# Order and place of VectorE work in the first two tiles of a retention block with a maxout feed-forward: scores behind conversion, weight sums sooner, w_out's sums off GpSimd

## The chip, the cores and the metric

The kernel runs on one core of one Trainium2 chip. A core has TensorE (matrix products, into the banks of PSUM), VectorE (in the profile DVE), ScalarE (ACT), GpSimd (POOL) and SyncE (SP), which here only issues DMAs. Each engine works through its own queue in order; they wait for each other by semaphores. The metric is device microseconds of one execution, as the median of several.

## The reference

Retention over (8, 8, 576, 64) inputs, whose output, seen as 4608 tokens of 512 features, goes into a maxout feed-forward of width 768:

```python
gamma = 1.0 - 2.0 ** (-5.0 - np.arange(H, dtype=np.float32))
Dmat = np.where(rel >= 0, gamma[:, None, None] ** rel[None, :, :], 0.0)
ret = scores * Dmat[None, :, :, :]          # scores = q k^T / sqrt(D)
attn = np.matmul(ret, v)                    # -> x: (B*S, H*D)
h = np.maximum(np.maximum(x @ w1, x @ w2), x @ w3)
out = h @ w_out
```

The weights arrive in float64. The kernel computes in float32, and converts them on the chip, from the bits.

## The kernel before

**Tiles.** The 4608 tokens are nine tiles of 512 tokens, each of four blocks of 128. `ffn(t)` (L818) is the feed-forward of tile t as a generator. The loop at the end (L979) runs it in twelve portions and, ahead of each, the steps that `steps(t + 1)` names for it: loads, transposes, `scores`, `state`, `values` of the blocks of the next tile. So TensorE's queue has the retention of tile t+1 between the products of tile t. All orders are written out by this program; nothing reorders them later.

**Tile 0** uses plain products, since the weights come in meanwhile. `units` (L482) are pairs (fp, i): fp is one of three pairs of 128-wide blocks of the hidden features, i one of the three weights. `up_plain` (L781) multiplies, and its `maximum` takes the result into h, on VectorE for i > 0. `convert(n)` runs n steps of `convert_all` (L616). A step issues one or a few of: the exponent's bits on VectorE (L632) and the mantissa's low half on ScalarE (L634); two ScalarE steps on the exponent (L640, L643) with the fraction's bits on VectorE (L641); the whole mantissa (L646); the sign (L650); and the product (L658), which is the float32 weight and which issues the loads of later pieces (`load_weights`). Pieces are worked in an overlapped order: the exponent step of a piece stands ahead of the sign and product of the piece before it. In the second unit, just behind the first block's products, `scores`, `state` and `keep` of block 4 are called (L829 to L832). `scores` (L277) issues the products of q and k to TensorE and the multiplication by a causal mask (L291, shown as L203) to VectorE; `keep` (L358) issues the new state there.

**From tile 1 on** both products use sums. The up products use a scheme with twenty products for each fp (`PRODUCTS`, L67), made of sums of x (`X_SUMS`) and of the weights (`W_SUMS`). The weight sums are made once: 19 VectorE subtractions or additions for each fp (L470), those of fp 0 at the end of tile 0, those of fp 2 and 1 during tile 1. They stand in the list `chores`. Work of the retention and sums of x stand in `urgent`. In `up` (L735) the chains A to E accumulate in PSUM banks; ScalarE copies the value of a chain after certain products (`part<-a` and so on, L747), and VectorE joins them (`JOINS`, L750). Chains C, D and E use two banks in turn, so D takes the bank of E, and the next E that of C; the joins that read e and c straight from PSUM free them.

For each TensorE step of `up` (40 for each fp: two for each product), `ffn` decides at L866 to L869 what VectorE gets next: an urgent step at step % 4 == 1, and at step % 4 == 3 if many wait; else, on even steps, one chore. The order of fp is 0, 2, 1.

**The down products** (`downs`, L531) use seven products in the banks x, y and z, called dx, dy and dz in the profile. They need sums of h (H, L527 to L529, part of them on GpSimd) and of w_out (To): T1 = b12 - b11 (L512), T2 = b22 - T1 (L513), b12 = b22 - b12 in place (L516), T4 = b21 - T2 (L517), each for three fp. T1 is used in product 5, T2 in product 6, b12 in product 7 and T4 in product 4. The order of the products is 1, 2, 6, 7, 5, 4, 3. The sums of w_out are made once, in tile 1, behind product 1 (L879). There is a step of the loop in `ffn` for each product; behind product 2 stands the sum that gives osb (L576).

Of the kernel before, what the change touches and what calls it, by code (L numbers as in the profile page):

```python
# [45 lines left out]
ALU = mybir.AluOpType  # L46
# [17 lines left out]
            b21 = b21 - b41, b42 = b42 - n5, b22 = b22 - b21, n6 = b31 + n2, b32 = b22 - b32, n8 = b12 - n4,  # L64
# [17 lines left out]
def kernel(  # L82
# [14 lines left out]
    nc = tc.nc  # L97
# [8 lines left out]
    CPT = NT // C  # L106
# [21 lines left out]
    def half(j):  # L128
        return slice(D * j, D * (j + 1))
# [31 lines left out]
    def start_of(g):  # L161
        r = -g * C % S
        return r if r < C else None
# [23 lines left out]
    late, chores, urgent, scaling, spread = {}, deque(), deque(), deque(), []  # L187

    def scale(n=1):
        for _ in range(min(n, len(scaling))):  # L190
            scaling.popleft()()  # L191

    def chore(n=1):
        for _ in range(n):
            if urgent or chores:
                (urgent or chores).popleft()()

    def soon(step):

        if spread:  # L200
            urgent.append(step)
        else:
            step()  # L203
# [73 lines left out]
    def scores(g):  # L277
        chore(len(urgent))
        scale(len(scaling))
        if g >= BY_CHUNKS:  # L280
            chunk_scores(g)
            return
        qT, kT = qks[g]["q"], qks[g]["k"]
        s = [ps_r.tile([C, NP, C], FP32, tag="r", name=f"s{j}") for j in range(2)]
        for p in range(NP):
            for j in range(2):
                r = slice(D * j, D * (j + 1))
                nc.tensor.matmul(s[j][:, p, :], lhsT=kT[r, p, :], rhs=qT[r, p, :], start=True, stop=True)
        for j in range(2):
            st = sts[g, j] = att.tile([C, NP, C], FP32, tag=f"m{j}", name="st", bufs=2 + j)  # L290
            soon(partial(nc.vector.tensor_tensor, st[:], s[j][:],  # L291
                         masks[start_of(g)][:].unsqueeze(1).to_broadcast([C, NP, C]), op=ALU.mult))

    def begins(g):
        return g + 1 < NG and start_of(g + 1) != 0
# [51 lines left out]
    def state(g):  # L347

        kr = raws["k", g]
        kvs[g] = None  # L350
        if begins(g):
            r = start_of(g) or 0
            kvs[g] = ps_r.tile([P, NP, D], FP32, tag="r", name="kv")
            for h in range(H):
                nc.tensor.matmul(kvs[g][half(h % 2), h // 2, :], lhsT=kr[r:, h, :], rhs=vds[g][r:, h, :],
                                 start=True, stop=True)

    def keep(g):  # L358
        factor = gs[:].unsqueeze(2).to_broadcast([P, NP, D])

        def step(t, kv):
            if start_of(g) is not None:
                nc.vector.tensor_tensor(t[:], kv[:], factor, op=ALU.mult)
            else:
                nc.vector.tensor_tensor(t[:], kv[:], states[g][:], op=ALU.add)
                (nc.gpsimd if g < CPT - 2 else nc.vector).tensor_tensor(t[:], t[:], factor, op=ALU.mult)

        if begins(g):
            t = states[g + 1] = ppool.tile([P, NP, D], FP32, tag="part", name="state")
            soon(partial(step, t, kvs[g]))  # L370
# [111 lines left out]
    units = [(fp, i) for fp in range(NF // 2) for i in range(3)]  # L482
# [21 lines left out]
    def sums_of_outs():  # L504

        pool = late["pool"]
        lo, hi = slice(0, DM // 2), slice(DM // 2, DM)
        b11, b12, b21, b22 = (w_out[:, :, e, r] for e in range(2) for r in (lo, hi))
        t1, t2, t4 = (pool.tile([P, NF // 2, DM // 2], FP32, name=f"To{n}")[:] for n in (1, 2, 4))

        def on_vector(fp):
            nc.vector.tensor_tensor(t1[:, fp], b12[:, fp], b11[:, fp], op=ALU.subtract)  # L512
            nc.vector.tensor_tensor(t2[:, fp], b22[:, fp], t1[:, fp], op=ALU.subtract)  # L513

        def on_gpsimd(fp):
            nc.gpsimd.tensor_tensor(b12[:, fp], b22[:, fp], b12[:, fp], op=ALU.subtract)  # L516
            nc.gpsimd.tensor_tensor(t4[:, fp], b21[:, fp], t2[:, fp], op=ALU.subtract)  # L517

        late["sums of T"] = [partial(on, fp) for on in (on_vector, on_gpsimd) for fp in (0, 2, 1)]
        late["T"] = {1: b11, 2: b21, 3: b22, 4: t4, 5: t1, 6: t2, 7: b12}  # L520
        late["S"] = {n: pool.tile([P, NF // 2, NH], FP32, name=f"H{n}") for n in (1, 2, 3, 4)}

# [201 lines left out]
    def late_room():  # L724
        pool = late["pool"]
        late["W"] = [pool.tile([P, NF, P], FP32, name=f"n{n}") for n in range(1, 9)]
        late["X"] = {n: pool.tile([P, NH], FP32, name=n)[:] for n in sorted({x[0] for x in X_SUMS})}
# [3 lines left out]
    def convert(n):  # L731
        for _ in range(n):
            next(converting, None)
# [66 lines left out]
    def first_ups(h):  # L800

        g = CPT - 1
        rest0, copy0 = up_plain(0, h, 0, 0, g * C)
        convert(2)
        state(g)
        convert(2)
        values([g])
        keep(g)
        convert(2)
        rest1, copy1 = up_plain(0, h, 1, 0, g * C)  # L810
        convert(2)
        for step in (rest0, copy0, rest1, copy1):
            step()
        decay(CPT)
        transposes(CPT)
        convert(4)

    def ffn(t):  # L818

        h = hpool.tile([P, NF, NT], FP32, tag="h", name="h")  # L820
        if t == 0:
            for fp, i in units:
                if (fp, i) == units[0]:
                    first_ups(h)
                    yield
                    continue
                for fb in (2 * fp, 2 * fp + 1):
                    maximum, = up_plain(t, h, fb, i)
                    if (fp, i, fb) == (*units[1], 0):  # L829
                        scores(CPT)  # L830
                        state(CPT)
                        keep(CPT)  # L832
                    if (fp, i) == units[-1] and fb % 2:
                        maximum()
                        convert(2)
                    else:
                        convert(4 if (fp, i) == units[1] else 2)
                        maximum()
                yield
            convert(3)  # L840
            for fb, _ in enumerate(downs_plain(t, h)):
                convert(2 if fb < 2 else 4 * len(pieces))
                if fb == 2:
                    while_converting.close()
                    late["pool"] = ctx.enter_context(tc.tile_pool(name="late", bufs=1))
                    late_room()
                    sums_of_outs()
                    weight_sums(0)
                elif fb == 3:
                    chore(len(chores))  # L850
                if fb in (1, 3):
                    yield
            yield
            return
        order = (0, 2, 1)
        if t == 1:
            spread.append(True)
            weight_sums(2)
            weight_sums(1)
        total = len(order) * 2 * len(PRODUCTS)  # L860
        count = parts = 0
        for fp in order:
            while fp not in summed_fp:
                chore()
            for step, _ in enumerate(up(t, h, fp)):
                if step % 4 == 1 or step % 4 == 3 and len(urgent) > (2 if t == 1 else 6):  # L866
                    chore(len(urgent) > 0)
                elif step % 2 == 0 and chores:
                    chores.popleft()()  # L869
                if step % 3 == 2:  # L870
                    scale()
                count += 1
                if count * (NF // 2 * 3) >= (parts + 1) * total:
                    parts += 1
                    yield
            sums_of_hidden(h, fp)
        chore(len(urgent))
        for n, _ in enumerate(downs(t, h, order)):
            if t == 1 and n == 0:  # L879
                for step in late["sums of T"]:  # L880
                    step()
            chore(4)
            scale(2)
            if n in (1, 3):
                yield
        yield
# [92 lines left out]
    for t in range(N // NT):  # L979
        work = ffn(t)  # L980
        for todo in steps(t + 1):
            for step in todo:
                step()
            next(work, None)
# [51 lines left out]
```

## Time and profile before

| what | us |
|---|---|
| median of three runs | 753.45 (753.13 to 753.48) |
| the profiled execution | 753.01 |
| its span, first to last instruction | 751.3 |
| TensorE busy | 743.1 |
| VectorE busy | 518.7 |
| ScalarE busy | 327.3 |
| GpSimd busy | 71.4 |
| tile 1, start of its up products to that of the next tile's | 123.97 to 205.5 |
| tile 2 | 205.5 to 284.4 |

Times in the trace are microseconds from the first instruction. PE is TensorE's products and PEld its weight loads, which run ahead of the products. The clock granted to TensorE is at full speed throughout. Busy shares are means over stages; the waits have to be read where they occur. The ends of TensorE's instructions in a trace are modelled, so a wait shows in full between the starts of weight loads rather than as idle time of PE. A row's line is that of the call which records the instruction; work that goes through `soon` or a list may carry the line where the list is worked off.

### The profile page before, as it was taken

The page shows a single profiled execution, that of the slowest core. Times are in us where ns is not written, and L with a number is a line of the kernel's source. Part 1 is how long each engine was busy: PE and PEld are TensorE (multiplying, and loading weights), DVE is VectorE, ACT ScalarE, POOL GpSimd, SP SyncE. Part 2 cuts the span into 40 slices and gives each one's busy share as a digit, 9 for nine tenths or more (in the row PEclk, how much of TensorE's full clock was granted, in tenths as well). Part 3 has the DMA queues.
Part 4 walks back from the last instruction along what each step waited for, and adds up shares of the span by engine and source line. Part 5 has one row for each costly group of instructions (what it writes and reads, how often), then busy time and mean ns, then how long its engine had stood idle before and what let it go on. Part 6 is the DMA issues. An engine that isn't in the chain of part 4 may idle for free.

```text
span 751.3 us, 16659 instructions
## 1 busy us (share of the span) xinstructions
PE 743.1 (99%) x6768; PEld 615.1 (82%) x6768; DVE 518.7 (69%) x878; ACT 327.3 (44%) x657; POOL 71.4 (10%) x91
## 2 busy tenths in 40 slices
PE   9999999999999999999999999999999999999998
PEld 7645546888788888888888888888888888888887
DVE  3898899898846765686667746775667656763662
ACT  3764533554145433644254335542554255414441
POOL 3000000002300100011010101010101010100000
PEclk9999999999999999999999999999999999999999
DMA  9996842504252514241333224242514151000001
GB/s 229 239 226 140 225 92 72 99 12 85 62 94 41 100 37 96 48 81 48 80 77 68 61 66 90 35 81 67 102 24 91 44 94 35 2 29 29 1 0 57
DMA packets 230206, 59.31 MB, mean 79 GB/s; under 512 B 210801, under 2 KB 228849, under 8 KB 230129
## 3 DMA queue, kind: packets, MB, share of 16 engines
q1 hardware_dynamic: 228720, 57.91, 35.6%
q8 instruction: 53, 0.87, 0.5%
q10 hardware_dynamic: 1408, 0.33, 0.2%
q14 instruction: 25, 0.20, 0.1%
HBM read 48.76 MB, written 9.44 MB: 77 GB/s over the span
## 4 chain that ended last, share of the span: by engine, by line
PE 90%; DVE 6%; SPq 2%; DMA 1%; issue 1%; ACT 0%; POOL 0%; DVEq 0%; POOLq 0%
PE a L762 18%; PE b L762 15%; PE dx L559 11%; PE c L762 8%; PE up L786 6%; PE dz L559 6%; PE d L762 5%; PE e L762 5%; PE sk L310 3%; PE down L773 3%; PE dy L559 2%; PE o L427 2%; PE o L434 1%; DVE part L750 1%; SPq L241 1%; DVE h L750 1%
## 5 line engine op out<-in xcount | busy, mean ns | idle before, releaser
L750 DVE TENSOR_TENSOR part<-part 128x512 f32<-128x512 f32 x168 | 116.0, 690 | 104.5 <-ACT part L747 102.0
L747 ACT COPY part<-b 128x512 f32<-128x512 f32 x120 | 70.3, 586 | 151.8 <-PE b L762 151.4
L750 DVE TENSOR_TENSOR h<-h,part 128x512 f32<-128x512 f32 x120 | 83.7, 698 | 29.5 <-ACT h L747 25.1
L747 ACT COPY part<-a 128x512 f32<-128x512 f32 x96 | 56.3, 586 | 51.2 <-PE a L762 50.8
L762 PE MATMUL a<-s,w 128*128 128x256 f32 x288 | 73.9, 379 | 0.0
L762 PE MATMUL b<-s,n 128*128 128x256 f32 x288 | 73.9, 379 | 0.0
L191 ACT ACTIVATE vraw<-vraw,gk 128x64 f32<-128x64 f32 x208 | 65.4, 346 | 0.5 <-DMA vraw<-in_v_dram 0.4
L786 PE MATMUL up<-xT,w 128*128 128x512 f32 (+2 forms) x160 | 64.2, 554 | 1.0 <-DVE w L658 1.0
L762 PEld LDWEIGHTS a<-s,w 128*128 128x128 f32 x288 | 54.7, 190 | 7.4
L762 PEld LDWEIGHTS b<-s,n 128*128 128x128 f32 x288 | 54.7, 190 | 7.4
L786 PEld LDWEIGHTS up<-xT,w 128*128 128x128 f32 x160 | 28.5, 190 | 31.3 <-issue 26.7
L327 POOL TENSOR_TENSOR s<-s,gs_of 64x512 f32<-64x512 f32 x21 | 22.3, 1062 | 318.1 <-DVE s L325 161.8
L762 PE MATMUL c<-xT,w 128*128 128x256 f32 x192 | 51.3, 389 | 0.0
L762 PE MATMUL d<-s,w 128*128 128x256 f32 x192 | 49.8, 380 | 0.0
L529 POOL TENSOR_TENSOR H<-h 128x256 f32<-128x256 f32 x24 | 20.2, 844 | 309.7 <-DVE h L750 305.3
L762 PE MATMUL b<-xT,n 128*128 128x256 f32 x192 | 49.3, 379 | 0.0
L559 PE MATMUL dx<-To,H 128*128 128x256 f32 (+1 forms) x204 | 45.4, 371 | 1.0 <-DVE To L513 1.0
L762 PE MATMUL e<-xT,w 128*128 128x256 f32 x192 | 45.4, 379 | 0.0
L762 PE MATMUL a<-xT,n 128*128 128x256 f32 x192 | 45.4, 379 | 0.0
L559 PEld LDWEIGHTS dx<-To,H 128*128 128x128 f32 x204 | 36.5, 190 | 6.6 <-DVE To L513 1.8
L762 PEld LDWEIGHTS e<-xT,w 128*128 128x128 f32 x192 | 36.5, 190 | 5.4 <-issue 0.5
L762 PEld LDWEIGHTS a<-xT,n 128*128 128x128 f32 x192 | 36.5, 190 | 5.0
(124 smaller groups left out, 1291.8 us busy)
## 6 DMA issues: line engine op xcount, KB each, us to landing
bits<-in_moe_w_dram SPq DMA_DIRECT2D x36, 256.0 KB, 6.0
out_dram<-osb SPq DMA_DIRECT2D x35, 256.0 KB, 2.1
kraw<-in_k_dram SPq DMA_DIRECT2D x32, 256.0 KB, 3.3
vraw<-in_v_dram SPq DMA_DIRECT2D x32, 256.0 KB, 3.9
qraw<-in_q_dram SPq DMA_DIRECT2D x224, 32.0 KB, 2.3
kxraw<-in_k_dram SPq DMA_DIRECT2D x224, 32.0 KB, 2.2
bits<-in_moe_w_out_dram SPq DMA_DIRECT2D x6, 512.0 KB, 5.5
qraw<-in_q_dram SPq DMA_DIRECT2D x6, 256.0 KB, 5.2
```

What stands on the lines that cost most here:

```text
L191: scaling.popleft()()
L241: nc.sync.dma_start(t[row:row + m], src[b, :, pos:pos + m, :].rearrange("h p d -> p h d"))
L310: nc.tensor.matmul(s[half(c), h, :], lhsT=kT[half(c), h, :], rhs=qT[half(c), h, :], start=True, stop=True)
L327: nc.gpsimd.tensor_tensor(new, new, factor, op=ALU.mult)
L427: nc.tensor.matmul(o[m][half(c), n, u, :], lhsT=vds[g][half(m), h, :], rhs=sts[g][half(m), h, :], start=n == 0 and u == 0, stop=place(g, m ...
L529: urgent.append(lambda: (pool(s3, a11, a21, op=ALU.subtract), pool(s4, a12, s2, op=ALU.subtract)))
L559: nc.tensor.matmul(o, lhsT=hS[n](fp)[:, m * P:(m + 1) * P], rhs=late["T"][n][:, fp, cols], start=first and fp == order[0] and (m == 0 or l ...
L747: nc.scalar.copy(of[step], ps[step[0]][:])
L750: nc.vector.tensor_tensor(of[dst], a, b, op=op)
L762: nc.tensor.matmul(ps[chain][:, e, :], lhsT=factor(w, 2 * fp + e), rhs=xS[t][x], start=n == 1 and e == 0, stop=ends, skip_group_check=True)
L773: nc.tensor.matmul(b[:], lhsT=h[:, fb, m * P:(m + 1) * P], rhs=w_sb["out", fb], start=(fb == 0), stop=(fb == NF - 1))
L786: nc.tensor.matmul(ps[:, a:b], lhsT=w_sb[i, fb][:, dc * P:(dc + 1) * P], rhs=xT[t][:, dc, a:b], start=dc == 0 and a == 0, stop=dc == NDC - ...
```

## The change

Three edits, all to the order or the engine of work that is there already.

1. In the second unit of tile 0, block 4's `scores`, `state` and `keep` are called behind the conversion steps and the maximum instead of ahead of them. TensorE's, ScalarE's and SP's queues keep their order; on VectorE two mask multiplications and one state multiplication move behind five conversion instructions and one maximum.
2. In the up products the condition for a chore loses `step % 2 == 0`. Chores now go at steps 0, 2 and, unless an urgent step goes there, 3 of every four. Only tile 1 has chores in this loop, so only its VectorE queue changes.
3. The twelve sums of w_out are all VectorE's. Those of T1 and T2 stand behind product 1, those of b12 and T4 behind product 6 (n == 2), each kind for fp 0, 2, 1 in turn. GpSimd loses six instructions.

```diff
-        def on_vector(fp):
-            nc.vector.tensor_tensor(t1[:, fp], b12[:, fp], b11[:, fp], op=ALU.subtract)
-            nc.vector.tensor_tensor(t2[:, fp], b22[:, fp], t1[:, fp], op=ALU.subtract)
-
-        def on_gpsimd(fp):
-            nc.gpsimd.tensor_tensor(b12[:, fp], b22[:, fp], b12[:, fp], op=ALU.subtract)
-            nc.gpsimd.tensor_tensor(t4[:, fp], b21[:, fp], t2[:, fp], op=ALU.subtract)
-
-        late["sums of T"] = [partial(on, fp) for on in (on_vector, on_gpsimd) for fp in (0, 2, 1)]
+        sums = ((t1, b12, b11), (t2, b22, t1)), ((b12, b22, b12), (t4, b21, t2))
+        late["sums of T"] = [partial(nc.vector.tensor_tensor, *(x[:, fp] for x in step), op=ALU.subtract)
+                             for steps in sums for step in steps for fp in (0, 2, 1)]
...
                     maximum, = up_plain(t, h, fb, i)
-                    if (fp, i, fb) == (*units[1], 0):
-                        scores(CPT)
-                        state(CPT)
-                        keep(CPT)
                     if (fp, i) == units[-1] and fb % 2:
                         maximum()
                         convert(2)
                     else:
                         convert(4 if (fp, i) == units[1] else 2)
                         maximum()
+                    if (fp, i, fb) == (*units[1], 0):
+                        scores(CPT)
+                        state(CPT)
+                        keep(CPT)
...
-                elif step % 2 == 0 and chores:
+                elif chores:
                     chores.popleft()()
...
-            if t == 1 and n == 0:
-                for step in late["sums of T"]:
+            if t == 1 and n in (0, 2):
+                for step in late["sums of T"][3 * n:3 * n + 6]:
                     step()
```

## The prediction

> **What bounds the kernel now.** I read the busy table and its slices first, then the waits of TensorE alone, then busy time by stretch, and last the order of time around each wait.
>
> ```profile
> PE 743.1 (99%) x6768; PEld 615.1 (82%) x6768; DVE 518.7 (69%) x878; ACT 327.3 (44%) x657; POOL 71.4 (10%) x91
> ...
> PE   9999999999999999999999999999999999999998
> ```
>
> TensorE works in every slice, so time can come only from its few waits. The waits of TensorE (who waited, on whom: us in total, times, longest):
>
> ```profile
> PE dx L559 <- DVE To L513: 1.0, 2, 0.6
> PE up L786 <- DVE w L658: 1.0, 1, 1.0
> PE sk L310 <- DVE qT L196: 0.9, 1, 0.9
> ```
>
> Each is a wait on VectorE (DVE), and each stands beside one part of the change. Busy time by stretch (stretch, its length, then PE, PEld, DVE, ACT, POOL): tile 1 in four pieces, and the whole of tile 2.
>
> ```profile
> 123.97:143.30 19.33, 19.33 (x194) 16.91 (x193) 16.08 (x34) 9.49 (x17) 0.00 (x0) 1.00 0.51 109
> 143.30:162.60 19.30, 19.30 (x193) 16.91 (x192) 19.07 (x38) 11.51 (x27) 2.86 (x3) 1.00 0.19 39
> 162.60:183.20 20.60, 19.75 (x209) 17.22 (x208) 17.62 (x30) 9.93 (x21) 4.32 (x4) 1.00 0.39 69
> 183.20:205.50 22.30, 21.27 (x215) 18.00 (x215) 18.94 (x35) 5.23 (x16) 6.82 (x8) 1.00 0.27 69
> ```
> ```profile
> 205.50:284.40 78.90, 78.90 (x806) 69.12 (x805) 52.05 (x88) 34.78 (x78) 7.80 (x9) 1.00 0.34 68
> ```
>
> Tile 1 takes 81.5 us where tile 2 takes 78.9, and from 205 us on TensorE never waits: tile 1 loses some 2.7 us. VectorE has 3.2 us to spare in the first piece and 0.2 in the second. Where the 2.7 go is seen in the weight loads (start, length, what):
>
> ```profile
> 190.75 0.73 PEld L559 LDWEIGHTS dx<-To,H 128*128 128x128 f32 x4
> 192.31 0.73 PEld L559 LDWEIGHTS dx<-To,H 128*128 128x128 f32 x4 [0.84 <-DVE To L513]
> 194.04 0.73 PEld L559 LDWEIGHTS dx<-To,H 128*128 128x128 f32 x4 [1.00 <-DVE To L513]
> 194.80 0.84 PEld L559 LDWEIGHTS dz<-w_out,H 128*128 128x128 f32 x4
> ```
>
> From the first load of dx to the first of dz is 4.05 us; in tile 2 the same stretch is 2.48 (271.13 to 273.61). So this wait costs 1.57, not the 1.0 of the list, as ends of matmuls are modelled. Likewise the scores of the second block stop at 169.86 and go on at 170.93: 1.07. Together 2.64, nearly all of the loss.
>
> **What the Trainium skill says.** "SBUF — State Buffer", Who interferes with whom: VectorE with two SBUF inputs and GpSimd share one pair of ports under an exclusive lock, and the loser waits for the whole instruction. The trace agrees: a 128x256 subtraction takes 0.41 us on VectorE alone, and 0.83 to 0.95 beside GpSimd (POOL) in these lines:
>
> ```profile
> 189.25 0.41 DVE L512 TENSOR_TENSOR To<-w_out 128x256 f32<-128x256 f32 x1
> 189.69 0.83 DVE L513 TENSOR_TENSOR To<-w_out,To 128x256 f32<-128x256 f32 x1
> 190.45 0.94 DVE L512 TENSOR_TENSOR To<-w_out 128x256 f32<-128x256 f32 x1
> ```
>
> "GPSIMD Engine Reference", Engine selection, calls GpSimd about twice as slow for such work: here 0.90 us (L516) against 0.41. Neither page bears on the order of a queue, which decides the other two parts.
>
> **Part 1, w_out's sums.** Removed: six GpSimd subtractions. Added: the same six on VectorE. Before, VectorE made T1, T2 for pair 0, then for 2, then 1, from 189.25 to 193.99, five of the six at 0.83 to 0.94 because GpSimd ran from 188.08 to 195.3. After, at the same place stand T1 for 0, 2, 1 and then T2 for 0, 2, 1. GpSimd keeps only its hidden sums (L529, to 190.24). T1(0) 189.25 to 189.66; T1(2) held by L529 as the line at 189.69 was, to 190.52; T1(1) to 190.87; T2(0) to 191.20; T2(2) and T2(1) each 0.335 later (the spacing of back-to-back sums in the trace), to 191.54 and 191.87. TensorE wants T2(0) at 190.75, gets it at 191.25, and needs the next 0.83 and 1.65 later: no further wait. Loss 0.50 in place of 1.57: gain 1.07. Bounds: T1(2) not held, T2(0) done at 190.7 and the gain 1.57; one more hold of 0.5, gain 0.57.
> The second group stands behind the sum into osb (0.68): b12 for three pairs from 192.4, the first done at 192.8; the product that reads it starts at 190.75 + 0.50 + 2.48 = 193.7. T4 is done by 194.6, read at about 198.9. So it is hidden; were osb a microsecond late, it would cost that less 0.9. xT follows at 194.5, as before, against a TensorE 1.1 us ahead; the product that first reads xT's sums starts at 207.1 - 1.1 and those sums are done within 2 us of xT.
>
> **Part 2, weight sums at three of four products.** Same 38 sums, earlier in VectorE's queue; TensorE's, ScalarE's and SP's orders don't move. In the order of the instructions, 23 of them, not 17, stand ahead of the three joins that start at 141.52. VectorE waits there for ScalarE's copies: 1.13 at 130.67, 0.89 at 133.26, 0.29 at 135.85 and 0.76 at 141.52, 3.07 in all. Six sums are 6 x 0.335 = 2.0: they fit, and the joins still start at 141.52. From there to the transpose at 170.17, without idle time, 15 sums remain of 21.
>
> ```profile
> 168.09 2.17 DVE L750 TENSOR_TENSOR h<-h,part 128x512 f32<-128x512 f32 x3
> 170.17 0.70 DVE L196 STREAM_TRANSPOSE qT<-qraw 128x512 f32<-128x512 f32 x1
> ```
>
> The transpose then runs from 168.15 to 168.85, and TensorE wants it at 169.86: the wait of 1.07 goes, with 1.0 to spare. Bounds: half the idle time filled gives just that, none gives 0. In between VectorE is later than before: 10 more sums stand ahead of the join that frees bank e (151.87 to 152.54), six absorbed, so it ends at 153.9, and product d, which takes that bank, starts at 154.51. Spare 0.6. The join of c at 157.22 is 0.7 later, its bank needed at 162.8. What is queued behind these sums, the xT sums and the transposes, is on time again from 158.5.
>
> **Part 3, block 4's scores behind the conversion.** Before, VectorE stood 2.61 us (to 37.12) for the scores, with conversion queued behind. After, two 0.335 steps, three 0.6 steps and a maximum fill that; the data landed by 33.07. VectorE is 2.5 us ahead at 43.83, but not for long: the next piece's bits land at 42.43, and the one after at 46.72 (landing marks in the trace). Its first step stands ahead of the product that TensorE awaits:
>
> ```profile
> 46.97 0.69 DVE L632 TENSOR_SCALAR expo<-bits 128x1024 int32<-128x1024 int32 x1
> 47.57 1.22 DVE L650 SCALAR_TENSOR_TENSOR expo<-bits,expo 128x1024 int32<-128x1024 int32 x1
> 48.83 1.23 DVE L658 TENSOR_TENSOR w<-mant,expo 128x1024 f32<-128x1024 f32 x1
> ```
>
> 46.97 becomes 46.75 at best: gain 0.2 of 1.03. No DMA's issue waits on the moved steps, and DMA is full there. Bounds 0 and 0.5. The masks end 0.5 later, at 38.9, and are read at 65.
>
> **Sum.** 1.07 + 1.07 + 0.2 = 2.35. The profiled run, 753.01 (span 751.3 and 1.7 around it), becomes 750.65. The median of the runs is 0.44 above the profiled one: 751.1.
>
> **Rivals.** (a) One of the two big waits stays, or comes back elsewhere in tile 1: gain 0.8 to 1.6, 751.8 to 752.6. For it: T1 before T2 puts four sums, not two, ahead of the first needed, and a second hold takes half the gain; against it, the spare 1.0 at the transpose. (b) Nothing moves: 752.6 to 753.9. The sums would have to find VectorE's idle time unusable, and T2 be as late as before; the four idle stretches, each directly behind a group of sums, speak against it. (c) Slower: VectorE cannot use its idle stretches for the crowded sums, and bank e comes late. Ten sums of 0.42, none absorbed or overlapped, make the join 4.2 late, and two holds by GpSimd of 0.5 each 5.2. Product d has 2.0 to spare (152.54 to 154.51), so it waits 3.2; the transpose gains nothing then, and parts 1 and 3 give 1.27 back: 753.45 + 3.2 - 1.27 = 755.4. It decides from 3.3 late on. Against it: the same sums for pair 0 run back to back at 0.335 from 110.3 to 116.8.
>
> **How the numbers follow.** The likeliest, both waits shrunk, has 0.70, and its own range is 750.3 (the best bounds, 1.57 + 1.07 + 0.5) to 751.8 (0.57 + 1.07 + 0). Rival (a) has 0.18, (b) 0.07, (c) 0.05. 0.2% is 1.5 us, about what a measurement can tell from no change, so faster is below 751.95: 0.70 and a good half of (a), 0.80; same is the rest of (a), and (b): 0.15; slower 0.05. The range 750.3 to 752.3 takes in the likeliest and most of (a).
>
> **What would show it.** TensorE's list of waits should have no transpose in tile 1; the wait for To should be one of about 0.5, with dx to dz at 3.0 or less; the wait for w at about 50 us should stay near 0.8. T and b12 rows should take 0.41 but for one or two. The joins near 141.5 should start where they did, and the join of e near 153.5. From there to the end the time per tile stays 78.8. I am wrong if d waits for bank e, if VectorE's idle time from 127 to 141.6 has not fallen from 3.1 to about 1, or if osb is late and b12 with it.

## The result, and the profile after

The changed kernel takes 750.53 us (median of six runs, 749.91 to 751.16) against 753.41 for the kernel before: ratio 0.9962, 95% interval 0.995 to 0.9975. The forecast was 751.1. The profiled execution took 750.43, which is 2.58 less than that of before (753.01), where 2.35 were forecast.

The waits of TensorE in the changed kernel (who waited, on whom: us in total, times, longest):

```profile
PE warm L158 <- POOL ident masks.py:199: 1.4, 1, 1.4
PE s L288 <- ACT qT L275: 0.7, 1, 0.7
PE dx L553 <- DVE To L875: 0.5, 1, 0.5
PE qt L274 <- DMA qraw<-in_q_dram: 0.3, 1, 0.3
PE up L780 <- DVE w L652: 0.3, 1, 0.3
```

Of the three waits on VectorE that the prediction started from, the one for the transpose (sk) is gone, that for To is halved, and that for the converted weight w went from 1.0 to 0.3. A wait of 0.3 for q's data is new; nothing in the change touches it. The windows of busy time (stretch, length, then PE, PEld, DVE, ACT, POOL), tile 1 in four pieces and then tile 2:

```profile
123.75:143.10 19.35, 19.35 (x193) 16.94 (x192) 18.05 (x40) 9.49 (x18) 0.00 (x0) 1.00 0.51 107
143.10:162.40 19.30, 19.30 (x193) 16.90 (x192) 18.44 (x36) 11.50 (x27) 5.75 (x3) 1.00 0.18 37
162.40:182.00 19.60, 19.60 (x210) 17.19 (x209) 16.00 (x26) 9.92 (x21) 4.32 (x4) 1.00 0.41 73
182.00:203.00 21.00, 20.47 (x214) 17.89 (x213) 18.64 (x41) 5.23 (x17) 1.80 (x2) 1.00 0.28 73
203.00:282.00 79.00, 79.00 (x806) 69.23 (x805) 52.17 (x88) 34.88 (x79) 7.79 (x9) 1.00 0.34 68
```

VectorE (third figure after the length) is 2.0 busier than before in the first piece, with six more instructions, and 1.6 less in the third. TensorE now fills the third piece, which had lost 0.85, and loses 0.53 in the fourth, where it lost 1.03. Tile 2 is what it was.

To place the gain exactly I use the starts of the first weight load of chain e in each fp, as the ends of products are modelled. The columns "fp 0" and "fp 2" run from one such start to the next. The "rest" column is fp 1 and the down products; in every later tile that stretch takes 39.84, so what stands above 39.84 is lost.

| kernel | tile 1's first e at | fp 0 | fp 2 | rest | lost in the rest |
|---|---|---|---|---|---|
| before | 123.38 | 19.70 | 19.49 | 42.59 | 2.75 |
| after | 122.98 | 19.70 | 19.49 | 40.41 | 0.57 |

The gain of 2.58 in the profiled executions is 0.40 ahead of tile 1 and 2.18 in it. Behind it both kernels need 546.1 to the end of the span (751.3 - 205.16 and 748.7 - 202.58): nothing else moved.

**Part 1's place.** In the kernel before, GpSimd's line beside the slow sum of 190.45 (shown in the prediction) is this:

```profile
190.21 0.90 POOL L516 TENSOR_TENSOR w_out<-w_out 128x256 f32<-128x256 f32 x1
```

It ends at 191.11 and VectorE's sum at 191.39, 0.28 later. Each of the five slow sums ends 0.28 after the GpSimd instruction beside it, as it would if VectorE got its inputs only when GpSimd was done. Order of time around w_out's sums after the change (start, us, engine, line, out<-in, count):

```profile
187.67 1.61 DVE L875 TENSOR_TENSOR To<-w_out 128x256 f32<-128x256 f32 x3
187.82 0.84 POOL L523 TENSOR_TENSOR H<-h,H 128x256 f32<-128x256 f32 x1 [0.36 <-DVE H L522]
...
189.21 1.08 DVE L875 TENSOR_TENSOR To<-w_out,To 128x256 f32<-128x256 f32 x3
189.74 2.46 PEld L553 LDWEIGHTS dx<-To,H 128*128 128x128 f32 x12 [0.64 <-issue]
...
190.21 0.68 DVE L570 TENSOR_TENSOR osb<-dy,part 128x512 f32<-128x512 f32 x1
190.81 1.08 DVE L875 TENSOR_TENSOR w_out<-w_out 128x256 f32<-128x256 f32 x3
...
191.81 1.08 DVE L875 TENSOR_TENSOR To<-w_out,To 128x256 f32<-128x256 f32 x3
192.22 2.56 PEld L553 LDWEIGHTS dz<-w_out,H 128*128 128x128 f32 x12
```

Three T1 beside GpSimd's last hidden sum take 1.61; the other groups of three, with GpSimd silent, 1.08. The twelve loads of dx, which were three groups of four with waits between them, are one row, and dx to dz is 2.48, the undisturbed length. One wait is left, ahead of the first load, for the first T2. The trace puts 0.64 ahead of that load down to "issue"; the list of waits has it as To.

**Part 2's place.** VectorE's order of time at its four idle stretches of fp 0, in brackets how long it stood, and for what:

```profile
130.27 0.69 DVE L744 TENSOR_TENSOR h<-h,part 128x512 f32<-128x512 f32 x1
...
132.86 0.69 DVE L744 TENSOR_TENSOR part<-part 128x512 f32<-128x512 f32 x1 [0.56 <-ACT part L741]
...
135.75 0.68 DVE L744 TENSOR_TENSOR part<-part 128x512 f32<-128x512 f32 x1
...
141.12 2.15 DVE L744 TENSOR_TENSOR part<-part 128x512 f32<-128x512 f32 x3 [0.49 <-ACT part L741]
```

The idle time at these four joins was 3.07; it is 0.11 (the view shows no bracket for so little) + 0.56 + 0 + 0.49 = 1.16. The triple of joins starts at 141.12, that is 0.4 earlier, as the whole tile is: it has not moved in the tile. Then the two rows that the prediction called critical, bank e's join with the product that takes the bank, and the transpose:

```profile
152.81 0.68 DVE L744 TENSOR_TENSOR part<-e,part 128x512 f32<-128x512 f32 x1
...
153.90 0.41 PEld L756 LDWEIGHTS d<-s,w 128*128 128x128 f32 x2
```
```profile
165.82 2.17 DVE L744 TENSOR_TENSOR h<-h,part 128x512 f32<-128x512 f32 x3
167.91 0.70 DVE L196 STREAM_TRANSPOSE qT<-qraw 128x512 f32<-128x512 f32 x1
```

The join ends at 153.49, 0.41 before d's first weight load and 0.62 before its first product (154.11). The transpose ends at 168.61; TensorE wanted it at 169.86 before, 169.46 after the shift of 0.4, so it is on time by 0.85.

**Part 3's place.** VectorE's conversion of the weight that TensorE waits for:

```profile
42.31 0.69 DVE L626 TENSOR_SCALAR expo<-bits 128x1024 int32<-128x1024 int32 x1 [0.82 <-DMA bits<-in_moe_w_dram]
...
46.56 0.69 DVE L626 TENSOR_SCALAR expo<-bits 128x1024 int32<-128x1024 int32 x1 [1.03 <-DMA bits<-in_moe_w_dram]
47.17 1.22 DVE L644 SCALAR_TENSOR_TENSOR expo<-bits,expo 128x1024 int32<-128x1024 int32 x1
48.43 1.22 DVE L652 TENSOR_TENSOR w<-mant,expo 128x1024 f32<-128x1024 f32 x1
```

VectorE is early, and stands twice for data: 0.82 for the piece that this weight is made from, and 1.03 for the next piece, which the weight doesn't need. That next piece landed at 46.44 here.

### The profile page after: what moved, and what is told of

Same layout as the page of the kernel before. It is cut to its first block, busy times and chain, and to the rows that moved or that the text cites. A ratio compares the mean times of both kernels' runs of the same rounds, so it can differ in the third digit from the quotient of the medians.

```text
span 748.7 us, 16661 instructions
## 1 busy us (share of the span) xinstructions
PE 742.2 (99%) x6768; PEld 615.2 (82%) x6768; DVE 518.5 (69%) x884; ACT 327.0 (44%) x657; POOL 69.2 (9%) x85
## 4 chain that ended last, share of the span: by engine, by line
PE 93%; DVE 3%; DMA 2%; SPq 1%; issue 0%; ACT 0%; DVEq 0%
PE a L756 19%; PE b L756 16%; PE dx L553 11%; PE c L756 9%; PE up L780 6%; PE d L756 6%; PE dz L553 6%; PE e L756 6%; PE sk L310 3%; PE down L767 3%; PE dy L553 2%; PE o L427 2%; PE o L434 2%; PE o L396 1%; DMA bits<-in_moe_w_dram 1%; PE s L288 1%
## 5 line engine op out<-in xcount | busy, mean ns | idle before, releaser
L327 POOL TENSOR_TENSOR s<-s,gs_of 64x512 f32<-64x512 f32 x21 | 22.3, 1063 | 321.3 <-DVE s L325 191.2
L756 PEld LDWEIGHTS b<-xT,n 128*128 128x128 f32 x192 | 36.5, 190 | 5.0
```

What stands on the lines that cost most here:

```text
L327: nc.gpsimd.tensor_tensor(new, new, factor, op=ALU.mult)
L756: nc.tensor.matmul(ps[chain][:, e, :], lhsT=factor(w, 2 * fp + e), rhs=xS[t][x], start=n == 1 and e == 0, stop=ends, skip_group_check=True)
```

## The experiments

My theory was the prediction's: three separate waits with three separate causes, of which part 1 takes the order of the sums and GpSimd's hold, part 2 the idle time of VectorE, and part 3 little, as the next piece's landing takes its place. The rivals: that the parts overlap (one of them makes up for another); that the order of the sums alone does what part 1 does, with GpSimd innocent; that part 2 stands close to an edge from which product d is late.

### Each part alone

Part 1 alone (the sums of w_out on VectorE, in two groups):

```diff
-        late["sums of T"] = [partial(on, fp) for on in (on_vector, on_gpsimd) for fp in (0, 2, 1)]
+        late["sums of T"] = [partial(nc.vector.tensor_tensor, *(x[:, fp] for x in step), op=ALU.subtract)
+                             for steps in sums for step in steps for fp in (0, 2, 1)]
...
-            if t == 1 and n == 0:
-                for step in late["sums of T"]:
+            if t == 1 and n in (0, 2):
+                for step in late["sums of T"][3 * n:3 * n + 6]:
```

> Only the twelve sums of w_out on VectorE in two groups; the rest as before. My theory (three separate waits, their gains add): the wait for To falls from 1.57 to about 0.55, so the time is 1.0 to 1.1 us below before (ratio 0.9986), the wait for the transpose (1.07) and the one for w (1.0) stay. Rival (the parts only work together, since a TensorE that is earlier or later shifts what it waits for): the To stretch gains clearly less or more than 1.0, or the sk wait changes by more than 0.3.

Measured: 752.25 against 753.14, ratio 0.9988 (0.9981 to 0.9994). TensorE's waits in it:

```profile
PE up L780 <- DVE w L652: 1.0, 1, 1.0
...
PE sk L310 <- DVE qT L196: 0.9, 1, 0.9
...
PE dx L553 <- DVE To L875: 0.5, 1, 0.5
```

The other two waits stand untouched, and the rest of tile 1 takes 41.60: 0.99 less than before.

Part 2 alone:

```diff
-                elif step % 2 == 0 and chores:
+                elif chores:
```

> Only the weight sums at three of four steps. My theory: the wait of the scores for the transpose goes, 1.07 us gained (ratio 0.9986), VectorE's idle time between 127 and 141.6 us falls from 3.1 to about 1.2, the wait for To stays at 1.57. Rival (VectorE cannot use its idle time, or the join of bank e becomes the wait): no gain, and a wait of product d at about 154 us.

Measured: 751.84, ratio 0.9982 (0.9974 to 0.999). Its list of waits:

```profile
PE dx L559 <- DVE To L513: 1.0, 2, 0.6
PE up L786 <- DVE w L658: 1.0, 1, 1.0
```

There is no wait for the transpose. The rest of tile 1 takes 41.42, 1.17 less; fp 0 and fp 2 keep 19.70 and 19.49, so bringing the sums forward costs TensorE nothing there.

Part 3 alone:

```diff
-                    if (fp, i, fb) == (*units[1], 0):
-                        scores(CPT)
-                        state(CPT)
-                        keep(CPT)
                     if (fp, i) == units[-1] and fb % 2:
...
+                    if (fp, i, fb) == (*units[1], 0):
+                        scores(CPT)
+                        state(CPT)
+                        keep(CPT)
                 yield
```

> Only block 4's scores behind the conversion. My theory: the weight that TensorE awaits at 49 us stands behind the landing of the next piece, so the gain is 0.2 to 0.4 us (ratio 0.9996), no more than the landing times allow. Rival (a queue of VectorE alone sets that weight): 1.0 us gained and no wait for w at all. Second rival (the 0.4 us seen in the changed kernel's profile come from DMA times that differ between executions): no gain, and the landing of that piece anywhere between 46.4 and 46.8.

Measured: 752.33, ratio 0.999 (0.9984 to 0.9997), so 0.8 less, with an interval of 0.2 to 1.2; my 0.2 to 0.4 lies at its low end. The rest of tile 1 is 42.59, as before. The wait for w in it:

```profile
PE up L786 <- DVE w L658: 0.6, 1, 0.6
```

The wait is smaller but not gone, so the first rival is out: VectorE's queue alone does not set that weight. What follows: in tile 1 parts 1 and 2 add, 0.99 + 1.17 = 2.16 against 2.18 together. The three timed gains, 0.9 + 1.3 + 0.8 = 3.0, agree with the 2.9 of the whole change, though each is uncertain by some 0.5. No overlap is seen.

### Parts 2 and 3, with w_out's sums left as they were

Both edits above on the kernel before; part 1 is left out.

> The chores and the scores as changed, w_out's sums as before (half of them on GpSimd). My theory: the complement of the first run of this call, 1.3 to 1.5 us below before (ratio 0.9981), with the wait for To at 1.57 in full. Rival: with VectorE less late in tile 1, To's wait is smaller by itself, and the time is within 0.4 us of the changed kernel.

Measured: 750.74, ratio 0.9966 (0.9954 to 0.9979). In the trace the rest of tile 1 takes 41.42, 1.00 more than with the whole change, and the wait for To is back at two times and 1.0 in the list. So in the trace part 1 is worth the same 1.0 behind parts 2 and 3. The time does not show it: I expected 1.3 to 1.5 below before, and the median is 2.4 below (1.6 to 3.5) and only 0.2 above the changed kernel's, as the rival's figure had it. The rival's reason, a smaller wait for To, is not in the trace. The profiled execution took 751.42, the longest of the five and 1.6 below before's; its start of tile 1 is 0.44 earlier and tile 1 is 1.17 shorter, which is all of it. Where the other four runs gained more can't be seen.

### Only the order of w_out's sums: b12 and T4 back on GpSimd

```diff
-        late["sums of T"] = [partial(nc.vector.tensor_tensor, *(x[:, fp] for x in step), op=ALU.subtract)
-                             for steps in sums for step in steps for fp in (0, 2, 1)]
+        late["sums of T"] = [partial(engine.tensor_tensor, *(x[:, fp] for x in step), op=ALU.subtract)
+                             for engine, steps in zip((nc.vector, nc.gpsimd), sums) for step in steps for fp in (0, 2, 1)]
```

This is on the changed kernel. b12 and T4 stand behind product 6 in the program, but GpSimd reaches them at once, as nothing else is in its queue.

> The changed kernel, but b12 and T4 back on GpSimd, with the changed order of T1 and T2. My theory (the ports shared with GpSimd make VectorE's sums slow): the sums of T2 take 0.83 to 0.94 again, the wait for To in all is 1.5 to 1.8 us, and the time 1.0 us above the changed kernel's (ratio to before 0.9976). Rival (the order and the place of the two groups bring the gain): the wait stays near 0.5.

Measured: 751.25, ratio 0.9978 (0.9968 to 0.9988). The wait for To, and the order of time in it:

```profile
PE dx L553 <- DVE To L875: 1.6, 1, 1.6
```
```profile
186.74 2.15 DVE L875 TENSOR_TENSOR To<-w_out 128x256 f32<-128x256 f32 x3
...
187.70 2.63 POOL L875 TENSOR_TENSOR w_out<-w_out 128x256 f32<-128x256 f32 x3
188.81 2.67 DVE L875 TENSOR_TENSOR To<-w_out,To 128x256 f32<-128x256 f32 x3
189.86 2.46 PEld L553 LDWEIGHTS dx<-To,H 128*128 128x128 f32 x12 [1.70 <-issue]
```

Three T1 take 2.15 instead of 1.61, three T2 2.67 instead of 1.08, because GpSimd's three sums run among them. The rest of tile 1 is 41.47, where parts 2 and 3 alone had 41.42: the whole of part 1's gain is gone, and the order by kind is worth nothing by itself. This settles the second rival: it is GpSimd's absence that pays. "SBUF — State Buffer", Who interferes with whom, of the Trainium skill (an exclusive lock on the ports that the two engines share) agrees with what is seen: 0.89 per T2 here, 0.36 with GpSimd silent. That the loser waits for a whole instruction the page says beside another mode of VectorE; for these sums the 0.28 found in the kernel before shows it.

### The other order: T1 and T2 in turn for each fp

```diff
-                             for steps in sums for step in steps for fp in (0, 2, 1)]
+                             for steps in sums for fp in (0, 2, 1) for step in steps]
```

> The changed kernel, but T1 and T2 (and b12 and T4) in turn for each fp instead of kind by kind. My theory (the 0.5 us of wait left is the order: four sums stand ahead of the T2 that TensorE needs first): no wait for To is left, the stretch from the end of the retention's products to dz is 2.5 us, and the time is 0.5 us below the changed kernel's (ratio to before 0.9956). Rival (the wait left is GpSimd's hidden sum holding the ports, whatever the order): the wait stays at 0.3 to 0.6.

Measured: 749.24, ratio 0.9951 (0.9938 to 0.9963). That is 1.3 below the changed kernel, where 0.5 was expected; the two intervals overlap, and the profiled execution (750.5) is the longest of its five, so the trace has to say what the order does. Order of time:

```profile
188.28 0.41 DVE L875 TENSOR_TENSOR To<-w_out 128x256 f32<-128x256 f32 x1
...
188.72 0.83 DVE L875 TENSOR_TENSOR To<-w_out,To 128x256 f32<-128x256 f32 x1
...
189.77 2.46 PEld L553 LDWEIGHTS dx<-To,H 128*128 128x128 f32 x12
```

The first T2 is done at 189.55, before TensorE comes for it at 189.77; the wait for To is gone from the list, and the rest of tile 1 takes 39.84, nothing lost. So the order alone removes the 0.57 that the changed kernel kept, the two sums for other fp that stand ahead of the first T2, although GpSimd holds one sum here too (the T2 of 0.83). The hold alone may be enough as well: in the changed kernel it makes the three T1 0.53 longer (1.61 for 1.08), nearly the whole wait. A run without the hold was not made.

### Crowding the weight sums further

```diff
                 elif chores:
-                    chores.popleft()()
+                    for _ in range(min(2, len(chores))):
+                        chores.popleft()()
```

> The changed kernel, but two weight sums at each step, so that all 38 stand ahead of the masks of tile 1's first scores. My theory (only VectorE's idle time hides them, 1.2 us of it is left): the three joins near 141 us start 3 to 4 us later, TensorE waits in tile 1 for 0.3 to 1.0 us, and the time is that much above the changed kernel's (ratio to before 0.9965 to 0.9975). Rival (sooner is never worse): same as the changed kernel, no new wait.

Measured: 750.02, ratio 0.9957 (0.9945 to 0.997): the same as the changed kernel, and not the loss that I expected. Order of time on VectorE and on TensorE's weight loads:

```profile
144.74 2.15 DVE L744 TENSOR_TENSOR part<-part 128x512 f32<-128x512 f32 x3
...
153.00 0.68 DVE L744 TENSOR_TENSOR part<-e,part 128x512 f32<-128x512 f32 x1
```
```profile
153.74 0.31 PEld L756 LDWEIGHTS d<-s,w 128*128 128x128 f32 x2
```

Counted from the first e of tile 1, the triple of joins starts 3.9 later than in the changed kernel (22.02 against 18.14), as it was meant to. But the join that frees bank e ends only 0.45 later (30.96 against 30.51), since sums that went earlier no longer stand behind the triple. The first weight load of d comes 0.1 later (31.02 against 30.92), and its first product is on time at 31.13 in both. So the spare at bank e is real and all but used up here, but the number of sums is fixed, and crowding can't push that join much further. The third rival needed it 3.3 later than before; it is 1.35 in the changed kernel and 1.8 here.

### The T1, T2, b12 and T4 sums as weight sums, ahead of the down products

```diff
             weight_sums(1)
+            chores.extend(late["sums of T"])
...
-            if t == 1 and n in (0, 2):
-                for step in late["sums of T"][3 * n:3 * n + 6]:
-                    step()
```

This loads part 2's spare time on purpose: twelve more sums stand ahead of the second transpose.

> The changed kernel, but the twelve sums of w_out as chores directly behind the weight sums, so in tile 1's second fp, ahead of the transposes. My theory (the transposes have about 1.0 us to spare, and VectorE 0.56 us of idle time there): twelve sums at 0.335 are 4.0, so the transpose comes 3.4 us later, the scores wait 2.4 to 2.8 us for it, the wait for To goes; the time is 2.0 us above the changed kernel's (ratio to before 0.999). Rival (what is made earlier is only hidden better): 0.5 below the changed kernel.

Measured: 753.62 over a wide 751.85 to 755.59, ratio 0.9997 (0.9988 to 1.0007). TensorE's longest wait in it:

```profile
PE sk L310 <- DVE qT L196: 2.3, 1, 2.3
```

The transpose starts at 171.05 instead of 167.91, and the rest of tile 1 takes 42.50: 2.66 lost, although the wait for To is gone. In the changed kernel the transpose had 0.85 to spare; 3.3 later in the tile (front 0.2 earlier) it is about 2.5 late. That is the price when the cover is gone. The median is 3.3 above the changed kernel's 750.3 on the same chip, where 2.0 was expected; the trace says 2.09 (2.66 less the 0.57 of To). The four runs with a granted clock of 1.0 (751.85 to 752.32, the profiled one among them) are some 1.75 above it; the eight longer ones (753.59 to 755.59) all show 0.998. So the order costs about 2, and the rest goes with the lower clock, whose cause stays open.

### The product that TensorE awaits ahead of the next piece's first step

```diff
-            if following:
+            if following and n > 4:
                 following.exponent(both)
             two.sign(both)
             yield
             two.product(both)
+            if n == 4:
+                following.exponent(both)
             yield
```

> The changed kernel, but in one place of the conversion the sign and product of a piece ahead of the next piece's exponent, so that the weight that TensorE awaits at 49 us no longer stands behind that piece's landing. My theory (with the scores out of the way, the landing sets that weight): the weight is done by 47.6, no wait for w is left, and the time is 0.3 us below the changed kernel's profile, less where the piece lands early. Rival (TensorE is held by something else there too, a later weight or a DMA): the wait moves to the next weight, no gain.

Measured: 749.57, ratio 0.9953 (0.994 to 0.9965). VectorE's order of time in it:

```profile
45.69 1.23 DVE L644 SCALAR_TENSOR_TENSOR expo<-bits,expo 128x1024 int32<-128x1024 int32 x1 [0.30 <-ACT expo L637]
46.95 1.22 DVE L652 TENSOR_TENSOR w<-mant,expo 128x1024 f32<-128x1024 f32 x1
48.10 0.69 DVE L626 TENSOR_SCALAR expo<-bits 128x1024 int32<-128x1024 int32 x1
```

The product no longer stands behind an instruction that waits for the next piece: w is done at 48.17 (I had expected 47.6), and TensorE waits for it no more. So the landing of a piece that isn't needed yet is what keeps the rest of this wait alive in the changed kernel.

### Both improvements, and the changed kernel once more

The order in turn and the product first, together:

> The changed kernel with both last edits: T1 and T2 in turn, and the awaited weight ahead of the next piece's exponent. My theory (both are waits of their own): no wait for To, none for w, tile 1's last fp and down products take 39.84 us as in any later tile; 0.8 us below the changed kernel (ratio to before 0.9945 to 0.9952). Rival (one wait hides the other): no better than the better of the two alone.

> The changed kernel itself, on the same chip as the two above. Ratio to before 0.9955 to 0.9970. The wait for w at 49 us is what remains between TensorE's arrival and the landing of the next piece plus 3.2 us, so anything from 0 to 1.0 by the landing; the wait for To 0.5; tile 1's last fp and down products 40.4.

Measured on one chip: 749.5 for both improvements (748.97 to 749.6; ratio 0.9945, 0.9933 to 0.9958) and 750.3 for the changed kernel (749.92 to 751.39; 0.9959, 0.9945 to 0.9973). The waits of TensorE with both:

```profile
PE warm L158 <- POOL ident masks.py:199: 1.4, 1, 1.4
PE s L288 <- ACT qT L275: 0.7, 1, 0.7
PE o L396 <- DVE st L203: 0.2, 1, 0.2
```

None of the three waits on VectorE is left in the list, and tile 1 loses nothing (39.84). The starts of weight loads still show 0.26 lost to w (next section): w ends at 49.39 here, 6.1 after the landing of its own piece at 43.30, as it ended 6.1 after that landing in the run before (42.09). That data is needed for w itself, so this rest is of another kind. The gain on the changed kernel is 0.8, as expected. The profiled execution is the shortest of all, and each of its five runs is below each of the changed kernel's, though the two intervals overlap. Against the order in turn alone (749.24, on another chip) no difference can be told.

### What sets part 3's gain

Eight profiled executions have part 3 and the conversion order of the changed kernel, three have neither part 3 nor any other edit near it. The score products of block 4 start at a time s in each, the last part of the next piece's data lands at a time l, and w ends as the table says. The last column is the time from s to tile 1's first e:

| kernel | s | l | w ends | listed wait | s to first e |
|---|---|---|---|---|---|
| before | 35.93 | 46.72 | 50.05 | 1.0 | 87.45 |
| part 1 alone | 36.56 | 46.59 | 50.65 | 1.0 | 87.42 |
| part 2 alone | 35.84 | 45.24 | 49.94 | 1.0 | 87.42 |
| after | 36.22 | 46.44 | 49.65 | 0.3 | 86.76 |
| part 3 alone | 35.78 | 46.31 | 49.52 | 0.6 | 87.07 |
| parts 2 and 3 | 36.04 | 46.38 | 49.61 | 0.5 | 86.90 |
| order in turn | 36.22 | 47.05 | 50.26 | 1.0 | 87.37 |
| crowded | 35.70 | 46.18 | 49.39 | 0.6 | 87.02 |
| T early | 36.45 | 46.19 | 49.45 | none | 86.33 |
| order, on GpSimd | 35.90 | 44.77 | 47.98 | none | 86.15 |
| after, once more | 36.11 | 46.31 | 49.52 | 0.3 | 86.74 |

Without part 3, w ends at s + 14.1, and the landing has no say: with part 2 alone it was 1.5 earlier than before and w only 0.1. With part 3, w ends at l + 3.2 in all eight. The last column is shortest, 86.15, where w ends earliest (order, on GpSimd); with the product first, where w ends as early after s (12.1), it is 86.16. In the other rows it is longer by just what w ends later than s + 12.8. So TensorE needs w at s + 12.8, and the wait costs more than the list says: 1.30 before, where 1.0 is listed. Part 3 exchanges this fixed 1.3 (1.27 to 1.30 in the three) for a wait that the landing decides: from 1.2 (landing at 47.05) to none, on the mean of the eight 0.64, a gain of 0.66.

## Why the prediction held, step by step

- **Part 1, "gain 1.07", a loss of 0.50 left of 1.57:** 0.99, and 0.57 left. Right, for the stated reasons: one hold by GpSimd's hidden sum (1.61 for the three T1), then TensorE waits once for the first T2 and no more. The experiment with b12 and T4 back on GpSimd shows that moving them is what pays, and the order in turn removes the rest of the wait. The second group was hidden: the first b12 is done at about 191.2, and dz starts at 192.22, 2.48 behind dx.
- **Part 2, "the wait of 1.07 goes, with 1.0 to spare":** 1.17 gained, 0.85 to spare. The steps held one by one: idle time of 3.07 to about 1 (1.16), the joins at 141.5 unmoved (141.12, with a tile 0.4 earlier), the join of bank e 1.36 later (1.35), and 0.6 to spare ahead of product d (0.62). Six sums at 0.335, 2.0 in all, went into the idle stretches, which shrank by 1.91; the transpose came 1.86 earlier in the tile.
- **Part 3, "46.97 becomes 46.75 at best: gain 0.2 of 1.03":** the mechanism was right, since the landing does replace the scores as what VectorE stands for, but the term was too small. The step took the landing of one execution, 46.72, as fixed; it lies between 44.77 and 47.05 in those above. It also took the wait from the list, 1.03, where the starts of weight loads show 1.30. The profiled execution of the changed kernel lost 0.69 less to w, and its s came 0.29 later, about as much as the new wait for q's data (0.3): that makes the 0.40 ahead of tile 1. Alone it timed at 0.8 (0.2 to 1.2), and the stated bound of 0.5 was too low as well: the eight executions give 0.1 to 1.3.
- **The sum, 2.35:** 2.58 in the profile: 0.99 + 1.17 with 0.02 of rounding, and 0.40 in the front. The other 0.3 by which the median came out below 751.1 is the 0.44 that I added for the runs over the profiled execution: here the median is only 0.10 above it. Those 0.44 were chance of one execution rather than a fixed distance. The total came out near the forecast although part 3 was mis-sized, since its miss in the profile, 0.2, is small against the sum.
- **Rivals.** (a) had one of the two big waits stay: the list of waits speaks against it, and each part alone takes its own. (b), nothing moves: no. (c), bank e late: the join was 1.35 later where 2.0 were to spare; even the crowded kernel reached only 1.8, and its product d was on time. Where the cover is really gone, it was the transpose that came late and not d, when twelve sums too many stood ahead of it.

## What to carry to other kernels

When a tightly filled engine waits for another that is busy only 69% of the time, look in that other's order of time for idle stretches ahead of the awaited instruction: work that stands behind them can be brought forward into them at no cost, as long as the next thing that it pushes back is not late; that thing has to be named and its spare counted. Small sums that are shared out between VectorE and GpSimd can slow down the very chain that they were to relieve; here they were faster on VectorE alone, in the order in which they are needed. An instruction that waits for data not yet needed must not stand ahead of one that the busy engine awaits: its landing differs from execution to execution, and a profile shows only one of them.

## What the runs showed that I had not expected

- The landing of the same part of the same weights, in kernels with the same DMA orders there, varied from 44.77 to 47.05 us. A step that stands on it gains or loses up to 1.2 us from one execution to the next.
- The stretches of tile 1 agree to 0.01 us from execution to execution (fp 0 at 19.69 or 19.70, fp 2 at 19.49 in every profile), while its start varied from 122.05 to 123.98 us: nearly all the scatter of a profile is in the front, where data come in. The time from s to tile 1's first e varies only with the wait for w.
- The list of waits understates what TensorE loses, by an amount that differs: 1.0 listed for 1.57 lost (To, in three groups of loads), 0.5 for 0.57 (To after the change), 0.9 for 1.17 (the transpose), 1.0 for 1.30 (w), 2.3 for 2.66 (the transpose with twelve sums more ahead of it).
- The hold works the other way too. With part 2, GpSimd's hidden sum at 153.89 takes 3.73 us, where it took 0.84 before: VectorE's crowded weight sums beside it stay at 0.41 each, and GpSimd is the one that stands. Part 2 alone shows the same, 3.72. It costs TensorE nothing (fp 2 keeps 19.49); the result is read in the down products, over 30 us later.
